# One core, attention, a dense layer and routed experts: the second head of the first pair loaded doubled, v read in long runs, 128-row transposes among the experts

## The chip, the cores and the metric

The program runs on one core of a Trainium2 chip. The metric is the device time of one execution in microseconds; several executions are taken and their median is given. A profile is one more execution, taken by the hardware profiler, with a record of each instruction on TensorE (PE, and PEld for its weight loads), VectorE (DVE), ScalarE (ACT), GpSimd (POOL) and of the DMA queue that SyncE (SP) fills.

## The reference, cut to what matters

Three stages follow one another. The first is attention over 16 heads (2 batches of 8), 768 positions, head size 64, where a query sees only the keys of its own bucket; a bucket is the pattern of signs of six projections.

```
mask = q_bucket[:, :, :, None] == k_bucket[:, :, None, :]
scores = scale * np.matmul(q, k.transpose(0, 1, 3, 2))
scores = np.where(mask, scores, -1000000000.0)
scores = scores - np.max(scores, axis=-1, keepdims=True)
attn = np.exp(scores)
attn = attn / (np.sum(attn, axis=-1, keepdims=True) + 1e-09)
return np.matmul(attn, v).astype(np.float32)
```

The second is a dense layer over the 1536 tokens: `h = np.maximum(x @ w_in, 0.0)` (512 to 2048), then `h * h @ w_out`. Its weights lie in memory as 64-bit numbers and are turned into 32-bit ones in the kernel. The third sends each token to one of 8 experts: logits are sorted, each expert takes at most 192 tokens, and an expert computes `np.maximum(x[mask] @ w1[e], 0.0) @ w2[e]` (512 to 1024 to 512).

## The kernel before

**A written order.** The class `Sched` collects operations with an engine, a duration that the author gives, dependences, a priority and the buffers that they take and free. `order()` plays them through on these durations, and the instructions are emitted in the order that comes out. So each engine's queue has a fixed order, and an instruction that waits holds back all that stands behind it on its engine. The numbers in `PR`, `MP`, `EP`, `RP`, `FP` and `PREP` are priorities; they move work in this order and do nothing else (smaller goes first; unit u has `u + PR[...]`, a pair's preparation on PE `12 * pr - PREP + PR["pe"]` and a little more for each step).

**Attention** (`attention`). The heads are worked in 8 pairs, each pair in 12 units of 128 queries, 96 units in all. A unit is: four matmuls into a score bank (`s_pe`, L578), row maximum (`mx`, DVE, L594), exponential with its sum (`ex`, ACT, L597), sum and reciprocal (L600 and L603), scaling (`nrm`, POOL, L606), six transposes on PE (`tp_pe`, L614) that ACT and DVE copy out as a high and a low part (L622, L626). Each third unit ends with twelve matmuls against v (`pv`, L635 and L636).

For the scores a head needs q and k transposed, in a high and a low part, with one-hot codes of the buckets in the lower 64 partitions. The first head of all (`first`) loads its q and k once, has them doubled on chip, and gets every part on the partitions where it belongs. Each pair (`pair`) loads q, k and v of two heads by DMA (L449) in runs of 64 numbers, 256 bytes; transposes both heads at once, so that one head's parts come out on 64 partitions and the other's on the other 64 (`t_act`, `t_dve`, L456 to L464); computes the signs (`bits_pe`, L486) and codes (`oh_pe`, L492; `oh_act`, L497 and L499); and then spreads the parts to where each head wants them with DMAs from one part of on-chip memory to another (`copies`, L259): seven for each head, except the first head of pair 0, which `first` made. There is one set of source buffers for these copies (`HL` and `oh`), so a later pair's codes can't be written before the earlier pair's copies have read theirs.

**The dense layer** (`mlp`). 32 steps over 128-wide slices of the hidden size and 768 tokens: `mlp1` (L802, 24 matmuls of 384 columns), `chain` (ACT, DVE, ACT, and POOL for the low part, L815), `mlp2` (L829, 18 matmuls of 512 columns). For each of 16 slices f of the weights `conv` turns the 64-bit words into 32-bit numbers with one operation on ACT (L776) and four on DVE (L778, L780, L782, L784), and `split` makes a high part on ACT (L790) and a low part on POOL (L792). Accumulators are added up by DVE at the end of each run of steps (L846). `AHEAD = 3` lets the weights be made three steps before their use.

**Routing and experts** (`Router`, `experts`). For each of 8 phases the router ranks tokens with comparisons on DVE and ACT (`g_dve`, L1353 to L1357) that PE adds up (`g_pe`, L1364, 6 to 12 matmuls of 8 columns for each comparison), finds a threshold over two small transposes (`x_pe`, L1409; `y_pe`, L1415, with 8 rows), and emits token numbers. An expert's 192 tokens are gathered as 128 rows and 64 rows (L1676), transposed (`xt_pe`, L1694 with 128 rows and L1696 with 64), and go through two layers (L1790 or L1748 and L1749, then L1861 to L1868), while weights for the next ones are loaded and split (L1644, L1646). Scattered stores (L1915) end it.

Of the kernel before, what the change touches and what calls it, by code (L numbers as in the profile page):

```python
# [81 lines left out]
class Sched:  # L82
# [24 lines left out]
    def order(self):  # L107
# [40 lines left out]
        def when(i):  # L148
            t = max(free[self.ops[i][0]], ready_at[i])
            if self.ops[i][11]:  # L150
                t = max(t, port)
            acq = self.ops[i][6]
            for j, r in enumerate(acq):
                c = acq[:j].count(r)
                x = res[r]
                t = max(t, inf if len(x) <= c else sorted(y[0] for y in x)[c] if c else min(y[0] for y in x))
            return t

        while left:
# [34 lines left out]
            if locks:  # L194
                port = t + dur
# [57 lines left out]
def attention(nc, S, ps, mem, ident, q, k, v, proj, pat, xhi, xlo):  # L253
# [184 lines left out]

    def pair(pr, cm):
# [7 lines left out]
        def load(nm):  # L447
            a = T["raw", pr, nm] = mem(S.unit(T["li", pr, nm], "raw" + nm), [6, 2, 64])
            nc.sync.dma_start(a, {"q": q, "k": k, "v": v}[nm][b, hh:hh + 2].rearrange("h (p j) d -> p j h d", p=128))  # L449
# [51 lines left out]
        def v_act(h):  # L501
            if h == 0:
                T["V", pr] = mem(S.unit(T["vi", pr], "V"), [6, 2, 2, 64], R)
            nc.scalar.activation(T["V", pr][:, :, h, h], T["raw", pr, "v"][:, :, h], AF.Copy)

        def v_pool(h):
            V = T["V", pr]
            nc.gpsimd.tensor_tensor(V[:, :, h, 1 - h], T["raw", pr, "v"][:, :, h], V[:, :, h, h].bitcast(F32), op=OP.subtract)
# [3 lines left out]
        def ld_add(nm):  # L512
            T["li", pr, nm] = s = S.add("SP", .62, lambda: load(nm), [T.get(("ci", "k", (pr - LDP[nm == "v"], 1)))], prio=-60 if pr == 0 and nm == "v" else base - 20, acq="raw" + nm)
            ld[nm] = S.add("DMA", 2.1, None, [s], prio=base - 20, lat=1.8)

        for nm in "qk":
            ld_add(nm)
        H, L, cps = {}, {}, {}

        def mk(nm, hf, x):  # L520
            T["t", nm, hf, pr] = a = S.add("PE", .327, lambda: tr(nm, hf), [ld[nm], H.get((nm, 0))], prio=prio(x) + PR["pe"], acq=["B"] + (["H" + nm] if hf == 0 else []), rel=[("raw" + nm, T["li", pr, nm])] if hf else ())
            b_ = S.add("ACT", .375, lambda: t_act(nm, hf), [a], prio=prio(x) + PR["pa"])
            c = S.add("DVE", .47, lambda: t_dve(nm, hf), [a, b_], prio=prio(x) + PR["pd"], rel=[("B", a)])
            H[nm, hf], L[nm, hf] = b_, c

        for i, (nm, hf) in enumerate((("q", 0), ("q", 1), ("k", 0), ("k", 1))):
            mk(nm, hf, i)

        def cps_add(nm, h, x, deps):
            s = S.add("SP", .62 * (3 if nm == "k" else 2), lambda: copies(nm, h), deps, prio=prio(x) - 40, acq=[nm + "c"] if nm != "oh" else ())  # L530
            T["ci", nm, (pr, h)] = s
            return S.add("DMA", 1.1 if nm == "oh" else 1.65, None, [s], prio=prio(x) - 40, lat=DL)

        def ci(h, *nms):
            return [T["ci", nm, (pr, h)] for nm in nms if pr or h]

        def give(r, a, deps):
            S.add("NONE", 0.0, None, [d for d in deps if d is not None], rel=[(r, a)])

        for h in range(2):  # L540
            for nm in "qk":
                cps[nm, h] = None if pr == h == 0 else cps_add(nm, h, 3 if h == 0 else XC, [H[nm, 0], H[nm, 1], L[nm, 0], L[nm, 1], *(ci(0, nm) if h else ())])
        bt = []
        for hf in range(2):
            T["b", hf, pr] = a0 = a = S.add("PE", .515, lambda hf=hf: bits_pe("q", hf, 0), [H["q", hf], L["q", hf], cm["m"], T["b", 0, pr] if hf else None], prio=prio(4 + hf) + PR["pe"], acq=["B"] + (["bits"] if hf == 0 else []), w=.3)
            a = S.add("PE", .515, lambda hf=hf: bits_pe("k", hf, 2), [H["k", hf], L["k", hf], a], prio=prio(4 + hf) + PR["pe"], w=.3)
            bt.append(S.add("DVE", .47, lambda hf=hf: bits_dve(hf), [a], prio=prio(4 + hf) + PR["pd"], rel=[("B", a0)]))
        for nm in "qk":
            give("H" + nm, T["t", nm, 0, pr], [*bt, cps[nm, 0], cps[nm, 1]])
        o, op = [], []  # L550
        for hf in range(2):
            for qk in range(2):
                x = 6 + 2 * hf + qk
                T["o", hf, qk, pr] = a = S.add("PE", .163, lambda hf=hf, qk=qk: oh_pe(hf, qk), [bt[hf], cm["m"], *op[:1]], prio=prio(x) + PR["pe"], acq=["B"] + (["Hoh"] if x == 6 else []), w=.3, half=1)
                op.append(a)
                o.append(S.add("ACT", .463, lambda hf=hf, qk=qk: oh_act(hf, qk), [a, cm["b"]], prio=prio(x) + PR["pa"], rel=[("B", a)]))
        give("bits", T["b", 0, pr], op)
        for h in range(2):
            cps["oh", h] = None if pr == h == 0 else cps_add("oh", h, 9 + h, [*o, *ci(h, "q", "k"), *(ci(0, "oh") if h else ())])
        give("Hoh", T["o", 0, 0, pr], [cps["oh", 0], cps["oh", 1]])  # L560
# [1481 lines left out]
```

## Time and profile before

| | |
|---|---|
| median of 3 runs | 770.28 us (769.77 to 772.06) |
| the profiled execution's own time | 773.7 us |
| its span, first to last instruction | 771.9 us |
| PE, DVE, ACT, POOL busy, share of the span | 97%, 73%, 58%, 52% |
| granted TensorE clock, mean over the span | 0.986 |

The profiled execution is one of many and 3.4 us longer than the median. In a timeline a row gives start, duration, engine, line and operation, what it writes and reads, how many alike stand together, and in brackets how long the engine had been idle before it and what ended that. Matmuls are pipelined: a PE duration runs over the start of the next, so the difference between two starts is the better price. In the chain of work that ended last a row gives start, length, engine, line and number of instructions. Rows of SP are the issuing of DMAs, not the transfers.

### The profile page before, as it was taken

To read this page: it belongs to the slowest core of one execution; us is meant where nothing else is said; L and a number is where in the kernel's file an instruction comes from. 1 tells how busy PE (TensorE), PEld (TensorE's weight loads), DVE (VectorE), ACT (ScalarE), POOL (GpSimd) and SP (SyncE) were. 2 spreads that over 40 slices of the span, in tenths; PEclk is the share of its full clock that TensorE was granted. 3 is DMA by queue.
4 is the path that set the end of the run, shared out by engine and by line. 5 is a ranking of instruction groups with operands and counts; after the bars stand their busy time and mean duration, and the time that the engine had idled before them with its cause. 6 is when DMAs were issued, how large, how long until landed. Compare 5 with 4: busy or idle time off the path is not lost.

```text
span 771.9 us, 13993 instructions
## 1 busy us (share of the span) xinstructions
PE 751.4 (97%) x4950; PEld 655.8 (85%) x4950; DVE 562.4 (73%) x1171; ACT 451.1 (58%) x900; POOL 399.7 (52%) x401
## 2 busy tenths in 40 slices
PE   8989999999999999999999999999999999999996
PEld 6768889879897899999999999999768888888885
DVE  5869989989899967831771484134897888888883
ACT  6969999989998855542343334224443543345772
POOL 2667778768788975752463365215921112222621
PEclk9999999999999999999999999999889999999998
DMA  6976586476640141410131110020136466478901
GB/s 157 244 165 144 115 175 150 102 159 143 157 103 2 56 164 64 153 57 1 55 113 51 53 58 1 0 82 28 56 114 235 154 229 212 152 259 312 349 26 37
DMA packets 87973, 94.33 MB, mean 122 GB/s; under 512 B 41920, under 2 KB 66880, under 8 KB 87904
## 3 DMA queue, kind: packets, MB, share of 16 engines
q1 hardware_dynamic: 85856, 87.16, 40.0%
q0 software_dynamic: 2048, 6.29, 2.6%
q8 instruction: 39, 0.64, 0.3%
q14 instruction: 30, 0.25, 0.1%
HBM read 63.55 MB, written 6.29 MB: 90 GB/s over the span
## 4 chain that ended last, share of the span: by engine, by line
PE 74%; DVE 8%; issue 5%; POOL 4%; ACT 4%; DMA 3%; SPq 1%; ACTq 0%; POOLq 0%; DVEq 0%
PE psS L829 11%; PE psTP L802 9%; PE psm L802 9%; PE psS L1790 6%; PE psS L578 4%; DVE p L626 3%; PE psTP L829 3%; PE psO L829 3%; PE psTP L614 2%; DVE f L594 2%; PE psS L1865 2%; PE psS L1861 2%; POOL f L606 2%; PE psS L1868 2%; PE psS L1862 2%
## 5 line engine op out<-in xcount | busy, mean ns | idle before, releaser
L606 POOL TENSOR_TENSOR f<-f 128x768 f32<-128x768 f32 x96 | 140.8, 1469 | 30.2 <-PE psTP L614 10.2
L815 POOL TENSOR_TENSOR r<-f,r 128x384 fp32r<-128x384 f32 x64 | 86.6, 1359 | 90.5 <-ACT r L813 77.9
L594 DVE TENSOR_REDUCE f<-psS 128x1 f32<-128x768 f32 x96 | 90.9, 948 | 7.6 <-PE psS L578 7.4
L829 PE MATMUL psS<-r 128*128 128x512 f32 x384 | 95.9, 395 | 0.0
L578 PE MATMUL psS<-r 128*128 128x384 f32 x384 | 88.4, 352 | 1.4 <-DMA r<-r 0.8
L597 ACT ACTIVATE f<-psS,f 128x768 f32<-128x768 f32 x96 | 87.1, 907 | 4.2 <-DVE f L603 1.4
L811 DVE TENSOR_TENSOR f<-f,psTP 128x384 f32<-128x384 f32 x32 | 17.7, 554 | 88.7 <-ACT f L809 88.4
L829 PEld LDWEIGHTS psS<-r 128*128 128x128 f32 x384 | 70.8, 188 | 13.1
L802 PE MATMUL psTP<-r 128*128 128x384 f32 x384 | 73.4, 338 | 0.7 <-POOL r L792 0.7
L802 PE MATMUL psm<-r 128*128 128x384 f32 x384 | 71.8, 334 | 0.0
L802 PEld LDWEIGHTS psTP<-r 128*128 128x128 f32 x384 | 67.9, 188 | 3.1 <-POOL r L792 1.0
L578 PEld LDWEIGHTS psS<-r 128*128 128x128 f32 x384 | 65.9, 190 | 5.3 <-ACT f L597 3.3
L802 PEld LDWEIGHTS psm<-r 128*128 128x128 f32 x384 | 67.1, 188 | 0.1
L1915 POOL DMA_INDIRECT out_dram<-ff,ix x16 | 17.9, 1116 | 83.8 <-DVE ff L1926 27.0
L1790 PE MATMUL psS<-ff,rf 128*128 128x192 f32 x320 | 61.0, 332 | 0.0
L626 DVE TENSOR_TENSOR p<-psTP,p 128x384 fp32r<-128x384 f32 x102 | 54.8, 546 | 4.9 <-ACT p L622 4.5
L813 ACT ACTIVATE r<-f 128x384 fp32r<-128x384 f32 x64 | 33.5, 523 | 39.3 <-DVE f L811 39.3
L1676 POOL DMA_INDIRECT ff<-x2d,ix x16 | 19.4, 1210 | 69.9 <-DVE ck L1549 17.7
L792 POOL TENSOR_TENSOR r<-f,r 128x1024 fp32r<-128x1024 f32 x16 | 40.4, 2526 | 28.4 <-ACT r L790 28.1
L1644 ACT ACTIVATE ff<-rf 128x1024 fp32r<-128x1024 f32 x32 | 33.8, 1055 | 34.8 <-PE psS L1863 25.2
L622 ACT ACTIVATE p<-psTP 128x384 fp32r<-128x384 f32 x102 | 49.3, 499 | 7.6 <-PE psTP L614 6.4
L1790 PEld LDWEIGHTS psS<-ff,rf 128*128 128x128 f32 x320 | 52.0, 190 | 1.9 <-DVE ff L1710 0.3
(400 smaller groups left out, 1860.9 us busy)
## 6 DMA issues: line engine op xcount, KB each, us to landing
rf<-in_moe_w_dram SPq DMA_DIRECT2D x64, 512.0 KB, 4.0
r<-r SPq DMA_DIRECT2D x90, 192.0 KB, 4.0
f<-in_moe_w_in_dram SPq DMA_DIRECT2D x16, 512.0 KB, 3.7
f<-in_moe_w_out_dram SPq DMA_DIRECT2D x16, 512.0 KB
r<-r SPq DMA_DIRECT2D x15, 384.0 KB
f<-in_q_dram SPq DMA_DIRECT2D x8, 384.0 KB
f<-in_k_dram SPq DMA_DIRECT2D x8, 384.0 KB
f<-in_v_dram SPq DMA_DIRECT2D x8, 384.0 KB, 3.8
```

Source lines behind the costliest of these rows:

```text
L578: nc.tensor.matmul(sbank(u)[:, hf, 0:384], T["q", (pr, h)][:, n, 128 * i:128 * i + 128], T["k", (pr, h)][:, n, 384 * hf:384 * hf + 384], s ...
L594: nc.vector.tensor_reduce(col(0, u), sbank(u)[:, :, 0:384], axis=AX.XY, op=OP.max, negate=True)
L597: nc.scalar.activation(P(u).rearrange("p (a b) -> p a b", a=2), sbank(u)[:, :, 0:384], AF.Exp, bias=col(0, u), accum_out=col(1, u))
L606: nc.gpsimd.tensor_tensor(Pn(u), P(u), col(3, u).to_broadcast([128, 768]), op=OP.mult)
L622: nc.scalar.activation(th, tp(u, g), AF.Copy)
L626: nc.vector.tensor_tensor(tl, tp(u, g), th.bitcast(F32), op=OP.subtract)
L792: nc.gpsimd.tensor_tensor(lo, F, hi.bitcast(F32), op=OP.subtract)
L802: nc.tensor.matmul(hbank(s, hf), w[:, c], y[:, x, sl], start=(c == 0 and i == 0), stop=(c == 3 and i == 2))
L815: nc.gpsimd.tensor_tensor(hl[:, sl], r, hh[:, sl].bitcast(F32), op=OP.subtract)
L829: nc.tensor.matmul(abank(i), a[:, t], w, start=(f == RUNS[r][1][0] and j == 0), stop=(f == RUNS[r][1][-1] and j == 2))
L1644: nc.scalar.activation(h(p, g, 0), w, AF.Copy)
L1790: nc.tensor.matmul(abank(n)[:, j], raw(p, g)[:, 0, 256 * c + 128 * j:256 * c + 128 * j + 128], xT(p)[:, c], start=(c == 0), stop=(c == 3))
```

## The change

- `pair(0)` makes no copies any more. A new function `second` loads q and k of head 1 with each run of 64 numbers doubled, transposes them so that both halves of the partitions hold the head, and writes each part where it belongs, as `first` does. The old path's joint transposes, signs and codes and its seven DMAs (L259) are no longer made for this pair.
- The raw v of every pair is laid out by head, so that a partition's run is 384 numbers, 1536 bytes, in place of 256 bytes.
- In `conv` the last operation on two tensors (comparing and multiplying, L784) goes; a maximum with a constant on one tensor comes in, ahead of the shift.
- For slices f from 10 on (`WLO`) and steps s from 14 on (`LOS`) the low parts are made by DVE, not by POOL.
- In `rank` the matmuls of two comparisons go out as one piece, save the last two.
- `y_pe` transposes all 128 rows, and `xt_pe` transposes the second gathered block with all 128 rows; its unused rows are set to zero once by POOL (`pad`).
- Assumed durations of DMAs are changed in the written order, a lock in it applies to more operations, and all priorities have other numbers, so that the order on every engine is a new one.

```
-PREP, PW, DL = -21, 0.8, 3.5
-PREP1 = 3
+PREP, PW, DL = -224, 0.8, 2.4
+PREP1 = 9.5
-PR = {"S": 10.5, "mx": 907, "ex": 577.5, "dn": -268.5, "rec": -506.5, "nrm": 32, "tp": 16, "hi": -161, "lo": -447.5, "pv": 16, "oa": 45.5, "od": 261, "pe": -93, "pa": -360, "pd": -559.5}
+PR = {"S": -6, "mx": 1033.5, "ex": 915, "dn": 242.5, "rec": -2168, "nrm": 581, "tp": -0.5, "hi": 240, "lo": -1372.5, "pv": 2, "oa": 1474, "od": 631.5, "pe": -246.5, "pa": 548.5, "pd": -695.5}
...
+    def second(cm):
...
+        def load(nm):
+            x = {"q": q, "k": k}[nm][0, 1].rearrange("(p j) d -> p j d", p=128)
+            nc.sync.dma_start(raw(nm), x[:, :, None, :].to_broadcast([128, 6, 2, 64]))
...
+        def hi(nm, hf):
+            o = kc() if nm == "k" else qc()
+            T[nm, (0, 1)] = o
+            nc.scalar.activation(o[:, 0, sl(hf)], tb(("t", nm, hf, 0)), AF.Copy, scale=1.0 if nm == "k" else 0.125)
+
+        def hi2(hf):
+            nc.scalar.activation(qc()[0:64, 1, sl(hf)], tb(("t", "q", hf, 0))[0:64], AF.Copy, scale=0.125)
...
+        def bpe(hf):
+            m = ((pf[:, 0], qc()[:, 0, sl(hf)]), (pf[:, 1], qc()[:, 0, sl(hf)]), (pf[:, 2], kc()[:, 0, sl(hf)]), (pf[0:64, 2], kc()[0:64, 1, sl(hf)]))
+            for i, (w, y) in enumerate(m):
+                nc.tensor.matmul(tb(("b", hf, 0))[0:32], w, y, start=(i == 0), stop=(i == 3))
...
+            if nm == "v":
+                nc.sync.dma_start(a.rearrange("p h j d -> p h (j d)"), x.rearrange("h (p j) d -> p h (j d)", p=128))
...
+        if pr == 0:
+            out = second(cm)
+        else:
...
-            return S.add("DMA", 1.1 if nm == "oh" else 1.65, None, [s], prio=prio(x) - 40, lat=DL)
+                return S.add("DMA", 1.85 if nm == "oh" else 2.75, None, [s], prio=prio(x) - 40, lat=DL)
...
+LOS, WLO = 14, 10
...
-            nc.scalar.activation(m, hw.bitcast(F32), AF.Abs)
+            nc.scalar.activation(t.bitcast(F32), hw.bitcast(F32), AF.Abs)
         elif j == 1:
-            V.tensor_scalar(t, hw, 3, 0x3FFFFFF8, op0=OP.logical_shift_left, op1=OP.bitwise_and)
+            V.tensor_scalar(t.bitcast(F32), t.bitcast(F32), LEAST, None, op0=OP.max)
         elif j == 2:
+            V.tensor_scalar(t, t, 3, 0x3FFFFFF8, op0=OP.logical_shift_left, op1=OP.bitwise_and)
+        elif j == 3:
             V.scalar_tensor_tensor(t, hw, -0x40000000, t, op0=OP.bitwise_and, op1=OP.bitwise_or)
-        elif j == 3:
-            V.scalar_tensor_tensor(t, lw, 29, t, op0=OP.logical_shift_right, op1=OP.bitwise_or)
         else:
-            V.scalar_tensor_tensor(m, m, LEAST, t.bitcast(F32), op0=OP.is_ge, op1=OP.mult)
+            V.scalar_tensor_tensor(m.bitcast(I32), lw, 29, t, op0=OP.logical_shift_right, op1=OP.bitwise_or)
...
-            nc.gpsimd.tensor_tensor(lo, F, hi.bitcast(F32), op=OP.subtract)
+            (nc.gpsimd if f < WLO else nc.vector).tensor_tensor(lo, F, hi.bitcast(F32), op=OP.subtract)
...
-            nc.gpsimd.tensor_tensor(hl[:, sl], r, hh[:, sl].bitcast(F32), op=OP.subtract)
+            (nc.gpsimd if s < LOS else nc.vector).tensor_tensor(hl[:, sl], r, hh[:, sl].bitcast(F32), op=OP.subtract)
...
+            pend.append((k, a))
+            if len(pend) == 2 or ds.index(k) >= len(ds) - LONE:
...
-            nc.tensor.transpose(T["xp"][:, 128:136], T["xm"][0:8].to_broadcast([8, 128]), self.ident[0:8, 0:8])
+            nc.tensor.transpose(T["xp"][:, 128:256], self.xm.to_broadcast([128, 128]), self.ident)
...
-                        nc.tensor.transpose(tv(q)[:, c, 128:192], g[1][0:64, 128 * cc:128 * cc + 128], ident[0:64, 0:64])
+                    nc.tensor.transpose(tv(q)[:, c, 128 * h:128 * h + 128], g[h][:, 128 * cc:128 * cc + 128], ident)
...
+    def pad():
+        for u in UNITS_F["xg"]:
+            nc.gpsimd.memset(mem(u + 2, [512])[64:128], 0.0)
+    T["pad"] = S.add("POOL", 1.0, pad, L, prio=-3)
```

## Rows read from the trace of the kernel before

**Rows 1.** Four stages: length, busy us of each engine, granted clock, DMA share, GB/s.
```profile
15.00:51.00 36.00, 32.11 (x191) 25.17 (x189) 26.64 (x54) 28.87 (x65) 19.44 (x24) 0.96 0.98 224
277.00:551.00 274.00, 273.62 (x1458) 249.78 (x1459) 144.42 (x186) 109.73 (x195) 138.12 (x99) 1.00 0.17 59
551.00:584.00 33.00, 30.32 (x439) 21.63 (x436) 27.94 (x77) 14.49 (x23) 11.05 (x11) 0.79 0.40 131
584.00:765.00 181.00, 180.97 (x1412) 155.55 (x1413) 148.16 (x422) 88.26 (x152) 44.55 (x54) 1.00 0.58 197
```

**Rows 2.** The chain that ended last, two steps of the dense layer, one period apart.
```profile
302.24 2.10 PE psTP L802 x12
...
310.55 2.10 PE psTP L802 x12
```

**Rows 3.** Row maxima (L594, one for each unit) in two stretches: DVE busy us, count.
```profile
15.00:50.30 35.30, 11.31 (x12) 0.96 0.98 224
65.40:217.30 151.90, 56.83 (x60) 1.00 0.66 146
```

**Rows 4.** Timeline of the stall at 45 us, on ACT, PE and DVE.
```profile
47.30 0.58 ACT L497 ACTIVATE r<-psTP,f 128x384 fp32r<-128x384 f32 x1 [2.49 <-DMA r<-r]
47.93 0.48 PE L492 MATMUL psTP<-f 128*128 128x384 bf16 x1 [2.49 <-ACT r L497]
50.36 0.96 DVE L594 TENSOR_REDUCE f<-psS 128x1 f32<-128x768 f32 x1 [3.86 <-PE psS L578]
```

**Rows 5.** Timeline of SP, which issues the DMAs, before 52 us.
```profile
22.77 11.84 SPq L259 DMA_DIRECT2D r<-r  x12
...
40.16 11.36 SPq L259 DMA_DIRECT2D r<-r  x11
```

**Rows 6.** Groups of DVE instructions by shape, whole span: busy us, mean ns.
```profile
L1646 DVE TENSOR_TENSOR ff<-rf,ff 128x1024 fp32r<-128x1024 f32 x32 | 39.1, 1222 | 7.2 <-ACT ff L1644 6.0 <-issue 0.6
L784 DVE SCALAR_TENSOR_TENSOR f<-f 128x1024 f32<-128x1024 f32 x16 | 26.3, 1645 | 0.2
L811 DVE TENSOR_TENSOR f<-f,psTP 128x384 f32<-128x384 f32 x32 | 17.7, 554 | 88.7 <-ACT f L809 88.4
L778 DVE TENSOR_SCALAR f<-f 128x1024 int32<-128x1024 int32 x16 | 15.2, 951 | 0.0
L846 DVE TENSOR_TENSOR f<-psS,f 128x512 f32<-128x512 f32 x16 | 10.6, 685 | 5.5 <-PE psS L829 5.4
```

**Rows 7.** Timeline: weight conversions on DVE; and POOL, L815 beside the last of them.
```profile
255.41 1.22 DVE L784 SCALAR_TENSOR_TENSOR f<-f 128x1024 f32<-128x1024 f32 x1
277.55 0.70 DVE L778 TENSOR_SCALAR f<-f 128x1024 int32<-128x1024 int32 x1
...
460.52 1.66 POOL L815 TENSOR_TENSOR r<-f,r 128x384 fp32r<-128x384 f32 x1 [0.29 <-ACT r L813]
461.34 1.92 DVE L784 SCALAR_TENSOR_TENSOR f<-f 128x1024 f32<-128x1024 f32 x1
```

**Rows 8.** The chain that ended last, in attention and among the experts.
```profile
242.47 0.33 PE psTP L614 x3
...
627.40 0.23 PE psS L1863
627.64 0.22 PE psTP L1364 x9
627.86 0.34 PE psS L1865
```

**Rows 9.** Timeline of PE, one expert's transposes with nothing between them.
```profile
650.56 0.38 PE L1694 MATMUL psO<-ident,ff 128*128 128x128 f32 x2
650.87 0.33 PE L1696 MATMUL psO<-ident,ff 64*128 64x64 f32 x2
651.05 0.28 PE L1696 MATMUL psm<-ident,ff 64*128 64x64 f32 x2
651.26 0.44 PE L1694 MATMUL psm<-ident,ff 128*128 128x128 f32 x2
```

More of the change, by code (lines that the diff above doesn't have):

```diff
@@ L537, in give @@
-        def give(r, a, deps):
-            S.add("NONE", 0.0, None, [d for d in deps if d is not None], rel=[(r, a)])
-        for h in range(2):
-            for nm in "qk":
[L542 to L556, printed above, removed]
@@ L567, in pair @@
             V.append(S.add("POOL", .97, lambda h=h: v_pool(h), [a], prio=prio(XV + h), rel=[("rawv", T["li", pr, "v"])] if h else ()))
-        T["end", pr] = [V[1], L["q", 1], L["k", 1]], [x for x in cps.values() if x is not None]
-        return {h: [cps[nm, h] for nm in ("q", "k", "oh")] if pr or h else cm["first"][0] for h in range(2)}, V
+        if pr == 0:
+            return (cm["first"][0], out), V
+        T["end", pr] = [V[1], L["q", 1], L["k", 1]], list(cps.values())
+        return {h: [cps[nm, h] for nm in ("q", "k", "oh")] for h in range(2)}, V
     def sbank(u):
@@ L907, in first @@
             c = S.add("ACT", .41, lambda s=s, hf=hf: chain(s, hf, 2), [b], prio=p(s, "ch"))
-            d = S.add("POOL", .956, lambda s=s, hf=hf: chain(s, hf, 3), [c], prio=p(s, "ch"))
+            d = S.add("POOL" if s < LOS else "DVE", .956 if s < LOS else .43, lambda s=s, hf=hf: chain(s, hf, 3), [c], prio=p(s, "ch" if s < LOS else "lw"), port=True)
             hd.append([c, d])
@@ L1078, in small @@
             P.memset(self.zero, 0.0)
+            P.memset(self.xm, 0.0)
             P.memset(self.ones, 1.0)
@@ L1357, in g_dve, with g_pe @@
                 V.tensor_scalar(G[:, 0:W], T["lr"], s, None, op0=OP.is_lt)
-        def g_pe(k):
+        def g_pe(ks):
             Rv = T["R"][:, 0:8 * n].rearrange("p (i e) -> p i e", e=8)
-            G = self.mem(T["G", k], [W], BF)
-            done.append(k)
-            for i in range(n):
-                nc.tensor.matmul(Rv[:, i], G[:, 128 * i:128 * i + 128], T["Bb"][:, k], start=False, stop=(len(done) == n and i == n - 1))
+            for k in ks:
+                G = self.mem(T["G", k], [W], BF)
+                done.append(k)
+                for i in range(n):
+                    nc.tensor.matmul(Rv[:, i], G[:, 128 * i:128 * i + 128], T["Bb"][:, k], start=False, stop=(len(done) == n and i == n - 1))
         act = ACT_TILES.get(n, ())
@@ L1369, in rank @@
         gt = None
+        pend = []
+        ds = [k for k in range(n) if k not in act]
         for k in [*act, *(k for k in range(n) if k not in act)]:
```

178 lines of the change are left out of this document (127 added, 51 removed).

## The prediction

> **What bounds the kernel now.** I read the busy time by stage first, then the chain of work that ended last, then the timelines of the stretches where that chain leaves PE. The stages [rows 1] show PE busy for 273.62 of 274.00 us in the dense layer and 180.97 of 181.00 us among the experts. Busy matmuls may hide waits, so the chain has to confirm it: in the dense layer it is PE all through, and one step repeats after 310.55 - 302.24 = 8.31 us [rows 2]. So in these 455 us a faster DVE, ACT or POOL gains nothing, and only PE's own work, or a wait that grows past the slack, can move the end. Between them, 551 to 584, PE is not the limit: the granted clock is 0.79 [rows 1], and the chain goes through comparisons, a gather and a weight load; nothing in the change takes an operation out of that path.
>
> Attention is another case. From 65.40 to 217.30 us it does 60 units in 151.90 us, 2.53 us each, and from 15.00 to 50.30 us 12 units in 35.30 us, 2.94 us each [rows 3]. At the later rate 12 units are 30.4 us, so the first pair loses 4.9 us. The timeline says where: PE's code matmul L492 waits 2.49 us for ACT L497, which waits for a copy between partitions; behind L492 in PE's queue stand the next units' scores, so DVE is without a row maximum for 3.86 us [rows 4]. The copy is late since SP and the transfers are full: 23 copies are issued in two runs of 11.84 and 11.36 us [rows 5], 1.01 us each, and the DMA engines are busy 0.98 of 15 to 51 us, at 224 GB/s [rows 1].
>
> **The change, part by part.** *Head 1 of pair 0 without copies.* Seven of the copies before 51 us go, at 1.01 us each 7.1 us of SP's queue, and with them their share of the full transfers. The doubled load issues as many DMAs of as many bytes as the joint load did. All later copies move up past these seven; the one that L497 waited for was late by 2.49 us, which is less than 7.1. So I take the stall as gone: -3.9 us, DVE's idle time, between nothing (another wait takes its place) and -4.9 us (all that the first pair loses). PE has four sign matmuls fewer, ACT two evictions more, under 1 us each; ACT has 36.00 - 28.87 = 7.1 us free in that stretch [rows 1], which hides it, and without that cover it would cost at most that 1 us. What could be late next is pair 1's own copies, still seven for each head, behind the pair's loads.
>
> *v in long runs.* As many bytes and as many DMAs. I count nothing: what a quicker v can gain in the first pair is inside the same 4.9 us, and a loss needs the longer runs to be slower, for which no row speaks.
>
> *Weight conversion.* Of four DVE operations one on two tensors, 1.22 us beside a POOL that hardly works, becomes one on a single tensor; the nearest row is L778 with 0.70 us [rows 7]: -0.52 us for each of 16 slices. Fourteen lie under PE in the dense layer and give nothing. Two fall into attention's end; 1.0 us at most, none if ACT or PE sets that stretch: I take -0.5 us. The raw buffer is freed one operation later, about 1.2 us against a lead of three steps of 8.31 us: nothing.
>
> *Low parts from POOL to DVE* (f from 10, s from 14). PE covers it: nothing, as long as DVE makes a slice within a step. What it costs if it doesn't is a rival below.
>
> *Pairs of comparisons.* A piece of L1364 costs 0.22 us and makes the matmul after it 0.34 instead of 0.23 us [rows 8], so each piece saved is worth 0.11 us. From 584 us on the written order has 36 pieces (two phases of 9, three of 6), then 24 (6 and 4): 12 x 0.11 = -1.3 us if each stands alone, nothing if neighbours stood together anyway. I take half, -0.7 us.
>
> *128-row transposes.* One expert's four groups now take, from start to start, 0.31, 0.18, 0.21 and 0.28 us [rows 9], 0.98 in all. Eight transposes of 128 rows at 0.33 / 3 = 0.11 us [rows 8] are 0.88; with the first group's surplus 0.31 - 0.22 and the last one's 0.28 - 0.22 it is 1.03: +0.05 us, times 8 experts +0.4 us. No row shows four such groups in a stay, so the ends are 0.18 and 0.31 for each later group: 0.85 to 1.24, or -1.0 to +2.1 us over 8 experts. The threshold's transpose (L1415) stays one instruction in each of 7 phases: nothing, and by the same surplus of 0.06 us at most 0.4 us either way. The zeroing on POOL comes ahead of the first gather; it is on the path only if POOL isn't free by then, and POOL is busy 11.05 of 33.00 us there [rows 1].
> The Trainium skill, TensorEngine Tiling (Array Packing), Key Properties, says that changing the tiling mode, and not just the tile, drains TensorE. By it both surpluses, 0.09 and 0.06 us, would be drains around the 64-row groups and would go, 8 x 0.15 = 1.2 us by these rows, and this term would be -0.8 instead of +0.4 us and the time 764.4; I give that 2 in 10. The trace shows no more than these surpluses, and shows the first also where L1364 hands over to an ordinary matmul, with no 64-row group near.
>
> *The new order.* Every priority changes, and no row prices that. A unit that gets 2% longer or shorter over the 78 units behind the first 18 is 78 x 0.05 = 4.0 us either way; this is my bound for it (an estimate), and I take nothing.
>
> Sum: -3.9 - 0.5 - 0.7 + 0.4 = -4.7 us. Against the profiled execution's 773.7 us (span 771.9 and 1.8 around it) that is 769.0; the median of the runs is 3.4 us below that execution, and from 770.28 it gives 765.6 us.
>
> **Rivals.** *More than the stall goes* (16%): the whole loss of the first pair, 1.0 us more, and a unit 2% shorter, 4.0 us: 760.6 us. For it: DMA 0.98 busy in the first pair and 0.66 later [rows 1, 3], so fewer bytes early should help all there. Against: the later units have no single large wait to remove.
>
> *Given back* (12%): the stall goes, but the new order makes the unit 2% longer: 769.6 us. For it: DVE and ACT are busy 26.64 and 28.87 of 36.00 us even in the stretch with the stall [rows 1], so a misplaced preparation costs on whichever is next. Against: the first pair's order was the only one with a large wait.
>
> *The change does not do what it says* (8%): codes still wait, since a later pair's codes need the one set of source buffers, whoever the first reader is: -0.8 us, 769.5 us. For it: the copies run in one unbroken line behind each other [rows 5]. Against: the line is seven shorter before the one that was late.
>
> *The stall moves* (7%): on PE a pair's preparation had priority 12 pr + 21 - 93 against a unit's u + 10.5, 82.5 units ahead, and now has 12 pr + 224 - 246.5 against u - 6, 16.5 ahead. If that makes copies late at a later pair, a wait of the same 3.9 us takes the old one's place, and a second follows: +3.1 us, 773.4 us. Against: 16.5 units are over a pair's 12, some 42 us.
>
> *DVE becomes the bound in the dense layer: slower* (8%). With one new slice in a step DVE would have, by the means of the trace, two single-tensor and two two-tensor operations (2 x 0.951 + 2 x 1.645), a low part of weights (1.222), and two products and two low parts of 128x384 (4 x 0.554): 8.63 us [rows 6] against a step of 8.31. That is 0.3 us for each of 6 slices, and six evictions of 0.685 at two ends of runs, 8.2 us: with 1.9 for the slices +10.1 us, or 775.7 us with the other terms. It decides from the point where DVE's share of a step passes 8.31 us. Against it: the means are those beside POOL. L784 is 1.92 us where POOL works on L815 and 1.22 where it hardly does [rows 7], and in these steps POOL has no such work left; with 0.70, 1.22, 1.22 and 0.554 the sum is 7.28 us.
> The Trainium skill, SBUF — State Buffer, Who interferes with whom, says that a DVE instruction with two inputs in that memory contends with a GpSimd one that reads it, the later of the two being fully blocked. The trace agrees in size, 1.92 against 1.22 us; by that rule the moved work takes its own obstacle away, which is why this rival has 8% and no more.
>
> **How the numbers follow.** The forecast keeps 49%; its own range is 761.6 to 767.9: below by the first term's other 1.0, half of the unit's 4.0 and 1.0 from the transposes, above to where no change begins. About 0.3%, 2.3 us, is what runs of this kernel can tell from no change. Faster by more (below 768.0): 49 + 16 = 65%. Within it: 12 + 8 = 20%. Slower (above 772.6): 7 + 8 = 15%. The range that should hold 8 in 10 takes in the forecast, both cases of no change, the moved stall, and most of the larger gain: 757.5 to 774.0; left out are the DVE case and the far end of the gain.
>
> **What would show it.** The first copy L259 belongs to pair 1, and no ACT L497 or PE L492 with an idle time of over 1 us before 55 us; the 13th row maximum starts near 46.5 us, not 50.36. Dense layer: period 8.31 us, PE without gaps; L784's successor about 0.7 us. Experts: 181 us become about 180.6. The prediction is wrong if the 60 later units take other than 151.9 us by more than 4, or if PE shows waits for weights between 440 and 520 us.

## The result and the profile after

The kernel after takes 757.38 us (median of 4 runs, 756.41 to 758.89) against 770.02 us of the kernel before (4 runs, 768.79 to 772.06): 12.6 us less, a ratio of 0.9838 with a 95% interval of 0.9822 to 0.9854. Forecast were 765.6 us and 4.7 us less. The time lies 0.1 us outside the range (757.5 to 774.0) and far outside the forecast's own range.

The stages of the kernel after, by windows; the columns are those of [rows 1]:

```profile
15.00:51.00 36.00, 34.78 (x216) 27.64 (x215) 32.18 (x67) 34.10 (x78) 26.05 (x32) 1.00 0.89 179
263.00:537.00 274.00, 273.91 (x1449) 249.48 (x1447) 146.55 (x226) 111.73 (x196) 70.61 (x58) 1.00 0.18 62
537.00:563.00 26.00, 24.56 (x427) 17.45 (x427) 23.96 (x66) 13.28 (x20) 9.81 (x13) 0.87 0.29 91
563.00:750.00 187.00, 185.18 (x1447) 161.55 (x1445) 151.90 (x436) 90.39 (x155) 44.70 (x55) 1.00 0.61 201
```

Row maxima of the kernel after (L687, before it L594), to be read against [rows 3]: DVE busy us and count, granted clock, DMA share, GB/s:

```profile
13.60:42.00 28.40, 11.33 (x12) 1.00 0.94 190
56.40:205.00 148.60, 56.57 (x60) 1.00 0.71 149
```

Twelve units take 28.40 us where they took 35.30, and 60 later ones 148.60 where they took 151.90 (35.0 and 150.8 in a second profile of the kernel before, below). In the first 36 us DVE and ACT do 32.18 and 34.10 us of work, against 26.64 and 28.87 [rows 1]. The transfers are still nearly full (0.89); they are no longer waited for. The dense layer is unchanged: the chain of work that ended last still has one step in 301.61 - 293.30 = 8.31 us, as in [rows 2].

```profile
293.30 4.18 PE psTP L896 x24
...
301.61 1.41 PE psTP L896 x8
```

The timeline of the conversions near 425 us, where POOL has nothing to do, shows L874 (the shift, now on one tensor) at 0.69 us, the two-tensor L876 at 1.22, and the low part L886, now on DVE, at 1.23:

```profile
425.52 1.23 DVE L886 TENSOR_TENSOR r<-f,r 128x1024 fp32r<-128x1024 f32 x1 [0.66 <-ACT r L884]
...
427.98 0.69 DVE L874 TENSOR_SCALAR f<-f 128x1024 int32<-128x1024 int32 x1
...
429.40 1.22 DVE L876 SCALAR_TENSOR_TENSOR f<-f 128x1024 int32<-128x1024 int32 x1
```

A second profile of the kernel before was taken with the experiments (771.45 us, span 769.7; expected as follows).

> The kernel before once more, for a second profile: 768 to 771 us. If the late start of the first profile (first row maximum at 15.1 us) was that execution's own: first row maximum near 13 us, the 13th near 47 us, and the stages after it as in the first profile within 0.5 us.

Its first row maximum starts at 14.9 us and its 13th at 49.9, so the expectation failed there. Between the 13th and the 79th it takes 166.0 us, 1.0 less than in the first profile, so a difference of 1 us between two profiles in such a stretch carries nothing by itself. The start differs between profiled executions: 13.0 us in run 11, whose order up to there is that of before, and 13.6 to 16.1 us in the runs that begin as after does (1, 6, 8 to 10, 12, 14 and 17). I therefore compare stretches and leave the start out. In the table, each number is the difference of two starts of row maxima, or of the ends and starts of the stages' matmuls, in one profiled execution (us). The numbers in the heads are those of the experiments below.

| | before (2nd profile) | after | old order, v first (7) | old attention order (15) | no second head (2) | before, new order (4) | conversion undone (8) |
|---|---|---|---|---|---|---|---|
| to the 1st row maximum | 14.9 | 13.7 | 13.5 | 14.0 | 13.0 | 12.6 | 13.7 |
| 12 units | 35.0 | 28.4 | 28.0 | 32.8 | 35.7 | 31.6 | 28.4 |
| 66 more units | 166.0 | 163.0 | 167.2 | 167.3 | 165.5 | 166.4 | 163.0 |
| of these, the last 60 | 150.8 | 148.6 | 152.3 | 152.2 | 148.8 | 148.8 | 148.6 |
| attention's end and dense layer | 332.3 | 331.2 | 333.9 | 334.6 | 331.2 | 337.4 | 337.4 |
| to the first expert matmul | 27.3 | 26.4 | 27.3 | 27.3 | 27.4 | 27.7 | 26.7 |
| expert matmuls | 187.9 | 186.7 | 187.3 | 185.7 | 186.0 | 187.5 | 187.6 |

From before to after: -6.6, -3.0, -1.1, -0.9 and -1.2, together -12.8 us without the start, which is what the medians say. Taken to the 19th row maximum, the first 18 units gain 7.3 us (50.1 to 42.8) and the last 60 of the row 2.2.

### The profile page after: what moved, and what is told of

It reads as the page before. It is cut to its first block, busy times and chain, and to the rows that moved or that the text cites. A ratio compares the mean times of both kernels' runs of the same rounds, so it can differ in the third digit from the quotient of the medians.

```text
span 755.7 us, 13988 instructions
## 1 busy us (share of the span) xinstructions
PE 740.3 (98%) x4955; PEld 652.8 (86%) x4955; DVE 562.8 (74%) x1213; ACT 454.9 (60%) x902; POOL 328.5 (43%) x362
## 4 chain that ended last, share of the span: by engine, by line
PE 76%; DVE 11%; ACT 4%; issue 3%; DMA 2%; POOL 2%; SPq 0%; POOLq 0%; ACTq 0%; DVEq 0%
PE psTP L896 17%; PE psS L923 12%; PE psS L1893 6%; DVE p L719 5%; PE psS L671 4%; PE psm L923 3%; PE psO L923 3%; DVE f L687 3%; PE psTP L707 2%; PE psO L707 2%; PE psS L1964 2%; PE psS L1968 2%; PE psS L1965 2%; PE psS L1971 2%; PE psS L1966 2%
## 5 line engine op out<-in xcount | busy, mean ns | idle before, releaser
L896 PE MATMUL psTP<-r 128*128 128x384 f32 x756 | 138.0, 336 | 0.0
L896 PEld LDWEIGHTS psTP<-r 128*128 128x128 f32 x756 | 132.3, 188 | 2.4 <-POOL r L886 0.2
L905 DVE TENSOR_TENSOR f<-f,psTP 128x384 f32<-128x384 f32 x63 | 34.9, 554 | 88.2 <-ACT f L903 88.1
L923 PE MATMUL psS<-r 128*128 128x512 f32 x384 | 100.3, 395 | 0.0
L687 DVE TENSOR_REDUCE f<-psS 128x1 f32<-128x768 f32 x96 | 90.6, 943 | 0.7 <-PE psS L671 0.5
L903 ACT ACTIVATE f<-psTP 128x384 f32<-128x384 f32 x63 | 31.0, 492 | 86.0 <-PE psTP L896 85.9
L1322 POOL TENSOR_SCALAR f<-f,mx 128x768 bf16<-128x768 f32 (+1 forms) x3 | 8.0, 2675 | 141.9 <-ACT f L1308 134.8
L719 DVE TENSOR_TENSOR p<-psTP,p 128x384 fp32r<-128x384 f32 x86 | 47.1, 549 | 5.4 <-ACT p L715 3.3
L909 POOL TENSOR_TENSOR r<-f,r 128x384 fp32r<-128x384 f32 x28 | 33.1, 1185 | 37.5 <-ACT r L907 29.2
L728 PE MATMUL psTP<-p,r 128*128 128x384 f32 x114 | 46.4, 407 | 0.5 <-DVE p L719 0.5
L715 ACT ACTIVATE p<-psTP 128x384 fp32r<-128x384 f32 x86 | 42.4, 496 | 5.0 <-PE psTP L707 4.3
```

The source lines that it names most:

```text
L687: nc.vector.tensor_reduce(col(0, u), sbank(u)[:, :, 0:384], axis=AX.XY, op=OP.max, negate=True)
L715: nc.scalar.activation(th, tp(u, g), AF.Copy)
L719: nc.vector.tensor_tensor(tl, tp(u, g), th.bitcast(F32), op=OP.subtract)
L728: nc.tensor.matmul(obank(g), w, th[:, c], start=(c == 0), stop=False)
L896: nc.tensor.matmul(hbank(s, hf), w[:, c], y[:, x, sl], start=(c == 0 and i == 0), stop=(c == 3 and i == 2))
L905: nc.vector.tensor_tensor(r, r, hbank(s, hf), op=OP.mult)
```

## The experiments

Times are medians; a ratio is to the kernel before on the same chip, with its 95% interval. Each "written order" is the one that the planner makes from priorities and assumed durations; an edit that the planner sees gives a new one on every engine.

### Which part carries it: second head and order, by halves

**1. v in short runs**, the order kept:

```
-            if nm == "v":
-                nc.sync.dma_start(a.rearrange("p h j d -> p h (j d)"), x.rearrange("h (p j) d -> p h (j d)", p=128))
+            nc.sync.dma_start(a, x.rearrange("h (p j) d -> p j h d", p=128))
```

> The kernel after, with v loaded in 256-byte runs again; the written order stays. Copies theory (the first pair's copies were the whole loss, v is small): 757.4 us as after, at most 1 us more, 13th row maximum at 42 us. Order theory (the new priorities gave most): 757.4 us too. v theory (the 256-byte runs of v crowd the transfers of the first 50 us): 760 us or more, 13th row maximum at 44 us or later.

757.87 us, 0.9852 [0.9839, 0.9864]: 0.5 us, not to be told from nothing. The longer runs of v are not the cause.

**2. The second head by copies again**, in the kernel after:

```
-        if pr == 0:
-            out = second(cm)
-        else:
+        if True:
```

> The kernel after, with pair 0 loaded, split and copied as before; the new priorities plan the order. Copies theory: the 9 us that the first 18 units gained go away, 765 to 768 us, 13th row maximum at 48 to 51 us. Order theory: 758 to 761 us, the 13th row maximum before 45 us. v theory: 760 us at most.

767.88 us, 0.9974 [0.9962, 0.9986]. Ten of the 12.6 us are gone, nearly all of them in the first 18 units (52.4 us against 42.8): the 60 later ones take 148.8 us and attention's end with the dense layer 331.2, as after. Its timeline has PE waiting in two places of the first pair (second and third field: length of the group, and in brackets the idle time before it):

```profile
30.33 1.30 PE L667 MATMUL psS<-r 128*128 128x384 f32 x3 [2.82 <-issue]
...
47.95 0.77 PE L667 MATMUL psS<-r 128*128 128x384 f32 x3 [2.69 <-DMA r<-r]
```

**3. The kernel after with all priorities and assumed times of before:**

```
-PREP, PW, DL = -224, 0.8, 2.4
-PREP1 = 9.5
+PREP, PW, DL = -21, 0.8, 3.5
+PREP1 = 3
```

and PR, MP, EP, RP, FP likewise.

> The kernel after, planned with the priorities and the assumed transfer times of before. Copies theory: 758 to 762 us, the 13th row maximum at 42 to 44 us, and only the 3.7 us of the later units go. Order theory: 765 to 770 us.

769.14 us, 0.9987 [0.9973, 1.0]. The copies theory fails: with every new instruction in place, the old order gives back all but 1 us.

**4. The reverse: the kernel before with the new priorities and assumed times**, no other edit.

> The kernel before, planned with the priorities and the assumed transfer times of after and nothing else of the change. Copies theory: 766 to 770 us, since the first pair's copies are all there. Order theory: 758 to 762 us.

771.01 us, 1.0024 [1.0007, 1.0041]. As an account of the total, the order theory fails as well. The scores of the second head wait for copies,

```profile
42.88 0.98 PE L578 MATMUL psS<-r 128*128 128x384 f32 x2 [2.22 <-DMA r<-r]
```

and attention's end with the dense layer takes 5.1 us more than before. Neither half alone shortens the whole by more than 1 us. But by the table the new order alone does shorten the 60 later units, to 148.8 us; the total hides that. And this run lacks the new conversion as well as the second head: run 8, which undoes the conversion alone, takes the same 337.4 us for attention's end and the dense layer. I formed a joint theory: each order has its own next wait, and both halves are needed to be rid of it.

**5. The second head alone**, in the kernel before (`second` as in the change, priorities of before).

> The kernel before with one part of the change: pair 0's second head by the doubled load, without copies; the priorities of before. Additive theory (the stall goes with the copies, whatever the order): 766 us or less, no wait over 2 us before 55 us. Joint theory (the old order puts another wait in its place, as in the run with the old priorities, where ACT waited 3.82 us for v): 767.5 to 770 us, with a wait of 2 to 4 us between 30 and 45 us.

768.3 us, 0.9981 [0.9965, 0.9998]: 1.5 us by the median, as the joint theory has it, but its 12 executions spread from 765.5 to 771.2. The profiled one was the quickest (765.51, span 763.7); in it 12 units take 29.6 us and the wait for v is 1.57 us, less than expected. So the spread leaves it open how much of the gain the old order eats in this kernel.

**6. Attention's parts alone**, in the kernel before: second head, long v, `PREP`, `PREP1`, `PR`, transfer times.

> The kernel before with the attention parts of the change (second head without copies, v in long runs, attention's new priorities and transfer times); the dense layer, the router and the experts as before. Joint theory: the second head and its order together carry about 10 us, 759.5 to 762 us, and the 13th row maximum starts by 45 us. Rival (the dense layer's and the experts' parts carry a third or more of the 12.6 us): 764 us or more.

765.73 us, 0.9942 [0.9927, 0.9957]. Between the two: the trace has 28.4 us for 12 units and 163.2 for the next 66, as after, so attention's gain is all there; then attention's end with the dense layer takes 335.3 us, 4.1 more than after and 3.0 more than before, and the experts 189.3, 2.6 more than after.

### What takes the stall's place under the old order

With the old priorities for attention (run 15), SP, ACT and PE near 40 us:

```profile
21.67 12.21 SPq L259 DMA_DIRECT2D r<-r  x12
33.93 0.67 SPq L535 DMA_DIRECT2D f<-in_v_dram  x1
...
40.00 0.52 ACT L592 ACTIVATE r<-f 128x384 fp32r<-128x384 f32 x1 [3.57 <-DMA f<-in_v_dram]
40.43 0.47 ACT L544 ACTIVATE r<-psm 128x384 fp32r<-128x384 f32 x1
...
40.95 0.54 PE L574 MATMUL psO<-r 128*32 128x384 f32 x2 [3.23 <-ACT r L544]
```

Pair 1's load of v stands on SP behind pair 1's twelve copies; issued at 33.93 it is awaited until 40.00. ACT, which works in order, stands still on rounding v (L592) for 3.57 us, and behind it the eviction L544, on which PE's sign matmuls (L574) wait 3.23 us. The same stall as [rows 4], at another place.

**7. That one load moved ahead of the copies**, in the kernel of run 3; no other instruction changes its place:

```
...
+        todo.remove(self.v1)
+        todo.insert(min(todo.index(i) for i in self.cp1), self.v1)
```

> The kernel after with the old priorities (769.1 us), and one DMA moved in its order: pair 1's load of v stands on SP ahead of pair 1's twelve copies, not behind them. If the wait of 3.82 us for v was what ate the gain of the second head: that wait is gone and the time falls by 3 to 5 us, 764 to 766 us. Rival (the transfers are full, so pair 1's copies land as late and something else waits for them): 768 to 770 us, with another wait of 2 to 4 us between 35 and 45 us.

765.27 us, 0.9922 [0.9906, 0.9938]: 3.9 us less than run 3 by one DMA's place.

```profile
13.35 2.42 SPq L539 DMA_DIRECT2D f<-in_v_dram  x1
21.17 13.54 SPq L263 DMA_DIRECT2D r<-r  x14
```

No wait of over 1.4 us is left between 10 and 60 us, and 12 units take 28.0 us. Shown: in the kernel of run 3 the wait for v had eaten these 3.9 us. In the kernel after, the copies of pair 1 start 5.2 us sooner than in run 15, so the load of v is issued 2.0 us sooner; and ACT comes to rounding v at 39.37 us, where in run 15 it stood ready for it from 36.43 (40.00 - 3.57). Had v taken as long to land as in run 15 (6.07 us from issue to use), it would have been there at about 38.0, an estimate; so the earlier issue and ACT's later turn do away with the wait together:

```profile
16.48 15.36 SPq L259 DMA_DIRECT2D r<-r  x12
31.89 0.77 SPq L535 DMA_DIRECT2D f<-in_v_dram  x1
...
39.37 0.51 ACT L592 ACTIVATE r<-f 128x384 fp32r<-128x384 f32 x1
```

### Which stage's order

**14. After, with the old priorities of dense layer, router and experts** (MP, EP, RP, FP).

> The kernel after with the priorities of the dense layer, the router and the experts of before; attention's stay new. If attention's order carries the gain: 757 to 760 us. If the later stages' order carries a third or more: 761.5 us or more, most of it lost between the 78th unit and the end of the dense layer.

757.74 us, 0.9833 [0.9809, 0.9858].

**15. After, with the old priorities and transfer times of attention** (PREP, PREP1, PR, DL, DMA times).

> The kernel after with attention's priorities and transfer times of before; those of the later stages stay new. If attention's order carries the gain: 766 to 769 us, 60 units in 151 to 152 us, a wait for v of 1.5 to 4 us near 36 us. If the later stages' order carries it: 762 us or less.

769.8 us, 0.9994 [0.9976, 1.0012]; 60 units take 152.2 us. Without attention's order nothing of the gain is left, and the later stages' priorities give nothing that can be measured. That does not make it the one carrier: without the second head 10.5 us go too (run 2), and with the conversion undone 7.6 (run 8, below). The parts need each other, so their prices don't add up.

### The conversion and the low parts

**8. Conversion and low parts undone, planned anew.**

```
-LOS, WLO = 14, 10
+LOS, WLO = 99, 99
```

and the four operations of `conv`, their releases and assumed durations as before. With them goes the planner's lock on these operations (it keeps DVE and POOL apart in the written order), which before holds for the first two slices alone.

> The kernel after with the weight conversion of before and all low parts on POOL again. If both lie under PE, as the prediction has it: 757.4 to 758.4 us, the dense layer's step 8.31 us in both. If the shorter conversion is part of the gain (attention's end, where PE isn't the bound): 759 to 761 us.

764.96 us, 0.9934 [0.9916, 0.9952]: 7.6 us more than after, and more than either theory. Up to the 84th unit the trace is that of after; the loss lies in attention's end and the first steps of the dense layer (337.4 us against 331.2).

**9. The old four operations in the places of the new ones**, every engine's order kept; low parts as after.

> The kernel after, its written order kept to the instruction on every engine, with the four conversion operations of before in the places of the new ones. If what the conversion gives is its own time on DVE (0.53 us a slice, two or three slices where DVE is full): 758.5 to 760 us. If the run with the conversion undone (764.96 us) lost by the instructions themselves: 763 us or more. If it lost by the order that was planned around them: 757.4 to 758.5 us.

758.39 us, 0.9854 [0.9829, 0.988]: 1.0 us by the medians, and the same by the stretch of attention's end and the dense layer (332.3 against 331.2). The same conversion costs 1.0 us in one order and 7.6 in another. Windows from 217 to 330 us of after, run 8 and run 9, in this order (each from its own profile):

```profile
217.00:330.00 113.00, 110.93 (x619) 101.27 (x618) 81.66 (x123) 74.80 (x141) 78.73 (x69) 1.00 0.25 85
```

```profile
217.00:330.00 113.00, 106.97 (x588) 95.08 (x587) 89.04 (x122) 71.99 (x137) 77.12 (x67) 1.00 0.25 85
```

```profile
217.00:330.00 113.00, 110.20 (x613) 100.25 (x613) 87.80 (x122) 74.63 (x140) 82.35 (x70) 1.00 0.25 85
```

PE is idle for 2.07, 6.03 and 2.80 us. DVE's work is nearly the same in runs 8 and 9 (89.04 and 87.80 us); what differs is the order, on DVE and on the others. (Run 8 has the low parts on POOL as well; run 10 prices that at 0.4 us.) Whether the order of run 8 is worse for the operations, their releases or the missing lock was not separated.

**10. Low parts on POOL again** (`LOS, WLO = 99, 99`), the new conversion kept.

> The kernel after with all low parts on POOL, as before (the order of the dense layer's second half is planned anew). If they lie under PE, as the prediction has it: 757.4 us, at most 0.7 us off. If the move to DVE is what the conversion's gain came from: 760 us or more, with PE waiting for weights.

757.75 us, 0.985 [0.9823, 0.9876]: nothing, as predicted, though DVE has 124.78 us of work between 263 and 537 us in place of 146.55; PE is busy 273.91 of 274 us in both.

**11. The new conversion alone, in the order of before.**

> The kernel before with the new conversion's four operations and nothing else; its written order stays. By the prediction's step: 769.3 us, 0.5 less than before, and no more than 1 us. If the shorter conversion is worth several us wherever DVE is full: 765 us or less. If it is worth something only together with attention's new order: 769 to 770 us.

783.86 us, 1.0192 [1.0164, 1.0219]: 14 us slower, and a miss of mine, not a price. The order of before issues the next slice's load ahead of the fourth operation, which in the new form still reads the raw slice's low words; so in this run it reads those of the next slice, and waits 4.91 us for their load:

```profile
327.53 1.23 DVE L784 SCALAR_TENSOR_TENSOR f<-f 128x1024 int32<-128x1024 int32 x1 [4.91 <-DMA f<-in_moe_w_out_dram]
```

**13. The same, its buffer declared free after the fourth operation**, planned anew with before's priorities.

> The kernel before with the new conversion, its raw buffer declared free after the fourth operation, so that the loads and the rest are planned anew with before's priorities. If the conversion is worth its own time: 768.5 to 769.5 us. If each new plan moves the time by several us either way, whatever the edit: 772 us or more, or 766 or less, with PE waiting between 230 and 350 us by more or less than before.

770.21 us, 1.0 [0.9986, 1.0014]: no gain that can be measured, nor any loss. Its 332.9 us for attention's end and dense layer are before's 332.3.

### Experts

**12. The 64-row transposes and the 8-row one of the threshold again.**

> The kernel after with the 64-row transposes of the gathered tokens and the 8-row transpose of the threshold as before. By the prediction's step (+0.4 us for the 128-row ones): 757 us. If the 64-row groups cost a drain of TensorE, as the prediction's other value has it: 758.2 us or a little more, and the experts' stretch 0.8 us or more longer.

758.56 us, 0.986 [0.9834, 0.9887]: 1.2 us by the median, within what the intervals of the two kernels leave open; the rows decide. One expert's eight transposes, first in after, then in this run:

```profile
680.87 0.60 PE L1799 MATMUL psTP<-ident,ff 128*128 128x128 f32 x4
681.31 0.60 PE L1799 MATMUL psm<-ident,ff 128*128 128x128 f32 x4
681.66 0.48 PE L1964 MATMUL psS<-ff,rf 128*128 128x512 f32 x1
```

```profile
683.22 0.38 PE L1800 MATMUL psTP<-ident,ff 128*128 128x128 f32 x2
683.52 0.34 PE L1802 MATMUL psTP<-ident,ff 64*128 64x64 f32 x2
683.70 0.28 PE L1802 MATMUL psm<-ident,ff 64*128 64x64 f32 x2
683.92 0.44 PE L1800 MATMUL psm<-ident,ff 128*128 128x128 f32 x2
684.11 0.49 PE L1967 MATMUL psS<-ff,rf 128*128 128x512 f32 x1
```

From start to start it is 681.66 - 680.87 = 0.79 us against 0.89: eight full transposes are quicker than four full and four half ones, by 0.10 us. So it is for the five experts whose eight stand together. For the other three they stand as two fours with other matmuls between, and there the difference is 0.21 to 0.28 us. Over all experts, from start to start, it is 7.97 us in this run against 6.76 in run 17, which has the transposes of after: 1.2 us, what the median says. The Trainium skill, TensorEngine Tiling (Array Packing), Key Properties, says that a change of tiling mode drains TensorE; these rows agree with it, with 0.10 us where an expert has one pair of changes (I had worked out 0.15 us from the surpluses) and about twice that where it has two, but no run separates a drain from another cost of the half-size ones.

**17. Comparisons one at a time** (`LONE = 99`).

> The kernel after with the matmuls of the comparisons one piece at a time, as before. By the prediction's step (-0.7 us for the pairs, between nothing and -1.3): 758.1 us, 757.4 to 758.7. If the pairs give nothing: 757.4 us.

757.79 us, 0.9849 [0.9829, 0.987]: 0.4 us, inside the measurement. The pairs are worth between nothing and 1 us, which leaves both expectations open.

## Why the prediction was wrong

**The step that failed is "The new order. Every priority changes, and no row prices that [...] I take nothing".** With all new instructions there, the new order is worth 7.9 us. The kernel of run 7 has every new instruction under the old order, with one load in a better place, and takes 765.27 us; with the new order it is 757.38. By the table, 3.7 us of that lie in the 60 later units (152.3 to 148.6) and 2.7 in attention's end and the dense layer; the first 18 units give none (42.8 us in both). I had bounded this term at 4.0 us, for the units alone, and then set it to zero in the forecast. The bound held for the units, but I had left out attention's end. There DVE is nearly full (12.74 of 13 us from 217 to 230 in after), and PE waits for what DVE does late. The longest such wait in run 7, and the same place in after:

```profile
240.66 1.22 DVE L884 SCALAR_TENSOR_TENSOR f<-f 128x1024 int32<-128x1024 int32 x1
...
243.25 0.95 DVE L693 TENSOR_REDUCE f<-psS 128x1 f32<-128x768 f32 x1
...
244.32 0.90 ACT L696 ACTIVATE f<-psS,f 128x768 f32<-128x768 f32 x1 [0.28 <-DVE f L693]
...
245.36 0.98 PE L677 MATMUL psS<-r 128*128 128x384 f32 x4 [2.35 <-ACT f L696]
```

```profile
239.38 0.96 PE L671 MATMUL psS<-r 128*128 128x384 f32 x4 [0.80 <-ACT f L690]
```

In run 7 DVE comes to a row maximum at 243.25 us, after a weight conversion (L884) and three evictions; the exponential waits for it, and PE's next scores wait 2.35 us for the exponential. In after that wait is 0.80 us.

Some 3 of the 7.9 us are no gain on the kernel before: under the old order the new instructions make the 60 later units 1.5 us and attention's end with the dense layer 1.6 us longer than before (152.3 against 150.8, 333.9 against 332.3). The second head alone does not do that (run 5: 150.7 and 332.4); which of the others does was not tried. So it is luck that run 7 comes within 0.4 us of the forecast: a first stretch better than forecast and later ones worse cancel in it.

**A second term was mis-sized, the first: -3.9, at most -4.9.** The first 18 units gain 7.3 us, with either order (runs 7 and after), more than "all that the first pair loses". The mechanism was right: the copy was late because SP and the transfers were full, seven copies went, and the wait went (no wait of 2.49 us is left near 45 us). The bound was wrong because it took the later units' 2.53 us as the least that a unit can take. The first units hold less work for PE, since transposes and matmuls against v come later than their scores. The second profile of before, and after, by instructions of PE:

```profile
14.80:49.80 35.00, 31.28 (x185) 24.17 (x184) 25.97 (x53) 28.40 (x64) 19.41 (x24) 0.96 1.00 226
```

```profile
13.60:42.00 28.40, 27.18 (x167) 20.50 (x166) 25.88 (x54) 26.58 (x59) 19.47 (x24) 1.00 0.94 190
56.40:205.00 148.60, 148.30 (x982) 132.76 (x981) 140.42 (x291) 140.93 (x318) 119.18 (x136) 1.00 0.71 149
```

The first 12 units of after hold 167, as many later ones 982 / 5 = 196; without a stall they take 28.0 to 28.4 us, not 30.4. They also hold 18 fewer than those of before, and half the matmuls against v (13 against 24), so part of the 6.6 us in the table's row of 12 units is work put off into the next row; the 19th row maximum is the fairer mark. By stretches the forecast was short by 3.4 us in the first 18 units, 2.2 in the 60 later ones, and 2.4 in all behind them.

**"More than the stall goes" (16%)** was the rival that came true, with more than its 5 us. I held against it that the later units have no single large wait to remove. That is right, and it did not matter: the new order shortens the 60 units by 2.2 us against the second profile of before, and does so without the second head and without the new conversion (148.8 us in run 2, which lacks the second head, and in run 4, which lacks both). PE from 57 to 205 us, in run 7 and in after:

```profile
57.00:205.00 148.00, 145.73 (x954) 129.03 (x953) 135.71 (x282) 136.33 (x307) 116.15 (x131) 1.00 0.69 146
```

```profile
57.00:205.00 148.00, 147.70 (x977) 132.16 (x976) 139.82 (x290) 140.33 (x316) 118.81 (x134) 1.00 0.71 148
```

PE's idle time falls from 2.27 to 0.30 us, which is about half of the 3.7 us between these two; where the rest lies, inside what counts as busy, is open. In the 60 units of before's second profile PE is idle for 1.07 of 150.9 us, so against that kernel idle time explains still less, 0.8 of the 2.2 us. My own sign of being wrong, 4 us in the 60 units, was too wide to see any of this.

**"The stall moves" (7%) and "The change does not do what it says" (8%)** were priced too low for what the second head does by itself. Under the old order the wait is back at the next late transfer: 3.57 us for pair 1's v (run 15), and 1.5 us are gained by the median (run 5). I had named pair 1's copies as what would be late next; it was its v, which SP issues behind those copies. My reading of the priorities, 16.5 units ahead against 82.5, told nothing of that.

**Conversion, -0.5 (at most -1.0):** 1.0 us where the order is kept (run 9), nothing where before's order is planned around it (run 13). The size is right; it hid that another plan around the old operations costs 6.6 us more (run 8 against run 9). **The raw buffer freed one operation later: nothing:** right once the plan knows of it (run 13).

**v in long runs, 0:** right within 0.5 us (run 1). **Low parts on DVE, 0:** right (run 10), and "DVE becomes the bound" did not come about: PE is busy for 273.91 of 274 us, and with POOL idle DVE's operations take 1.22 and 0.69 us as in [rows 7]. From 355 us on, all 16 conversions on two tensors take 1.21 to 1.23 us; in run 10, with the low parts on POOL, 4 of these 16 take 1.58 to 1.85. The Trainium skill, SBUF — State Buffer, Who interferes with whom, which I had weighed against that rival, agrees with this: the move took away what was left of its own obstacle, after the written order had kept the other 12 at 1.21 to 1.23 us even in run 10.

**Pairs of comparisons, -0.7:** 0.4 in run 17, not to be told from nothing. **Transposes, +0.4:** the sign was wrong; -1.2 by the median and by the rows of run 12, outside my -1.0 to +2.1. I gave the value -0.8 two chances in ten, though the only rows that had four such groups in a stay (0.98 us in [rows 9]) stood above eight full ones at 0.11; I then added surpluses to the full ones that they do not have.

**Right in the list of what would show it:** the first L259 belongs to pair 1, the successors of L497 and L492 have no idle time of over 0.5 us before 55 us, the period is 8.31 us, the shift takes 0.69 us. Wrong: the 13th row maximum starts at 42.1, not near 46.5, and 60 units take 148.6, not 151.9 (150.8 in the second profile of before).

What stays open: which of the new priorities does it (runs 14 and 15 narrow it to attention's, not further), and which new instruction makes the later units longer under the old order.

## What to carry to other kernels

In a kernel whose order is planned, price an edit twice, in the order as it stands and after a new plan: the old conversion cost 1.0 us in one order and 7.6 in another, and the second head gave 1.5 us (by the median) under the old order and 10.5 under the new. Before the rate of one stretch is taken as the bound of another, count the bounding engine's instructions in both, and look for small waits in the average: here 12 first units held 167 instructions where later ones held 196, and an order could take another 2.2 us off 60 units that showed no large wait. A total can hide a gain and a loss: run 4 gained 3.0 us in attention's first 78 units and lost 5.1 behind them. When a late transfer is removed, look in the issuing queue for what stands behind it: a load behind twelve copies was the next to be late, and moving it alone was worth 3.9 us by the medians.

## What the runs showed of the hardware

A stall on PE costs more than its length. In run 2 PE is busy for 2.48 of the 6 us from 24 to 30, and from 30 to 36 the granted clock is 0.50, the lower of the two levels (1.2 GHz); PE is then busy for 5.67 us over 18 instructions, 0.32 us each, where in the first window, at 2.4 GHz, it needed 8.89 us for 54, 0.16 each (not all of one kind; four matmuls of scores, L667, take 1.74 us at 34.74 and 0.86 at 22.08). The stall of [rows 4] did the same: the granted clock is 0.82 from 48 to 57 us of before, and 1.00 in after. Columns as in [rows 1]; the last row is of before:

```profile
15.00:24.00 9.00, 8.89 (x54) 6.38 (x53) 7.68 (x17) 8.23 (x21) 6.37 (x8) 1.00 1.09 233
24.00:30.00 6.00, 2.48 (x16) 1.47 (x13) 3.58 (x9) 3.43 (x9) 5.43 (x7) 0.96 1.04 214
30.00:36.00 6.00, 5.67 (x18) 4.29 (x19) 2.63 (x4) 2.87 (x6) 0.38 (x2) 0.50 1.03 236
```

```profile
48.00:57.00 9.00, 8.42 (x47) 7.54 (x47) 5.85 (x12) 7.82 (x18) 5.62 (x6) 0.82 0.65 140
```

And four half-size transposes among full ones are slower than full ones throughout: 0.89 against 0.79 us for eight in a row, and 0.21 to 0.28 us more where the eight stand as two fours (run 12).
